# Eight more idle matmuls on TensorE in the first block of a gated linear attention with a bilinear feed-forward

## The chip, the core and the metric

The kernel runs on one core of a Trainium2 chip. A core has five engines, each with its own instruction queue: TensorE (PE in the profile; its weight loads are PEld), VectorE (DVE), ScalarE (ACT), GpSimd (POOL) and SyncE (SP). The metric is the device time of one execution in microseconds (us), as the median of several runs. The profile shows one execution on its own.

## The reference

Gated linear attention over 4 batch rows, 8 heads, 768 steps and a head size of 48 comes first, then a bilinear feed-forward layer over the 3072 tokens with a model size of 384 and an inner size of 1536. `alpha` lies between 0.8 and 1.

```python
state = np.zeros((B, H, D, D))
for t in range(S):
    state = alpha[:, :, t, :, None] * state + np.einsum('bhd,bhe->bhde', k[:, :, t], v[:, :, t])
    y[:, :, t] = np.einsum('bhd,bhde->bhe', q[:, :, t], state)
x = y.transpose(0, 2, 1, 3).reshape(B * S, H * D)
out = (x @ w_a) * (x @ w_b) @ w_out
```

## The kernel before

The steps in time are cut into three stretches of 256 steps and the batch into two pairs of rows. So there are six blocks, numbered 0 to 5; block c has stretch c // 2 and the pair c % 2. Each block runs through the same stages for its two rows (u = 0 and 1):

- load alpha, q, k, v (`load`, line 547), logarithm of alpha on ScalarE (`ln`, line 554)
- running sums of the logarithms over the steps, by matmuls with a triangular matrix (`B`, lines 589 and 590, for block 0), and sums over half stretches for the decay of the state (`dk`, line 698)
- exponentials of the sums and of the negated sums on ScalarE (`E`, line 665), multiplied into q and k on VectorE (`mq`, `mk`, line 676)
- transposes of q and k on TensorE (`C`, line 736) and the copy of the result out of PSUM (`Ce`, line 960)
- scores of keys and queries (`D`, line 837), masked on VectorE (`M`, line 846) or copied by ScalarE and masked afterwards (`Mc`, line 850, and `Mm`, line 854)
- the state that is carried on: matmuls of keys and values (`K`, line 792) and its update with the decay on VectorE (`k`, lines 819 to 823); the decays are made by ScalarE (`de`, line 719)
- the output: carried part from the state (`SB`, `SA`) and inner part from the masked scores (`Y`), all through line 866, then the evacuation to `xT` (`X`, lines 902 and 904)
- feed-forward: `a` and `b` are the products with w_a and w_b (line 921), `as` copies one of them out on ScalarE (line 927), `pr` multiplies them on VectorE (line 935), `o` is the product with w_out (line 943); the last blocks use a scheme with fewer products (line 1032)

Values of the logarithm and the running sums of block 0 are float32, so their matmuls run as two passes each. Blocks overlap: while one is in its feed-forward part, the next is in its attention part.

The order of all work is written out by hand in the string `PROGRAM`. Each entry is an operation, with its arguments and, where there is a choice, the engine's letter (V is VectorE, S ScalarE, P GpSimd, Y SyncE). The loop at line 1142 issues them in this order, and each engine keeps it in its own queue, so an operation that must wait holds up all that stands behind it on the same engine. For matmuls one of the arguments is the number of the PSUM bank, 0 to 7, that they write; two-bank operations take the next one as well.

The operation `fill n i` (line 570) issues n matmuls of a 128x128 block of zeros with 128x512 zeros into bank i. Nothing reads what they write; a real operation overwrites it later. The tile of zeros, `wz`, is set once at the start. In the kernel before there are two places with such fills: seven at the very start, before alpha has landed, and two in block 0 between the transposes `C 0 1 3` and `C 0 0 1`. `B 0b`, `B 0a`, `B 1a` and `B 1b` are the running sums of block 0: row 0 or 1, each for half of the heads (a is heads 0 to 3, b is heads 4 to 7).

The loads of all weights (`W`, line 527, and `Wo`, line 530) and those of q, k, v and alpha marked P are issued by GpSimd, one behind the other and between its own work; those marked Y by SyncE.

Of the kernel before, what the change touches and what calls it, by code (L numbers as in the profile page):

```python
# [17 lines left out]
0: cm 0; c1; cz 0 b P; ci; ld a 0b Y; c1a; ld a 0a Y; ln 0b; cu; cz 1 b P; fill 7 0; cu2 V  # L18
0: cz 0 q V; cus; ld k 0b Y; ld k 0a Y; B 0b 2; ld q 0b Y; ln 0a; B 0a 0; ld v 0 P; ld q 0a Y; ld a 1 P; cs 0 m P
0: E 0b i; mk 0b V; ld k 1 P; ld q 1 P; cm 1; W b 0 256; cz 0 v P; E 0b b; mq 0b V; ld v 1 P; W a 256 768; dk 0 2  # L20
0: C 0 1 3; E 0a i; mk 0a V; cz 1 q P; E 0a b; mq 0a V; v 0 S; Ce 0 1 V; fill 2 0; W a 0 256; de 0; W b 256 512
0: C 0 0 1; Ce 0 0 V; D 0 1 2; K 0 0 0; vs 0 0 S; W b 512 768; cs 1 m P
1: ld a 0 P
0: D 0 0 4; k 0 0 V; SB 0 0; M 0 0; ln 1; B 1a 6
1: ld a 1 P
0: W a 768 1536; c2 P; W b 768 1536; E 1a i; E 1a b; B 1b 4
1: ld q 0 P
# [1150 lines left out]
```

## Time and profile before

| | us |
|---|---|
| median of 3 runs | 189.28 |
| the three runs | 189.28, 190.45, 189.12 |
| the profiled execution, own time | 190.44 |
| its span, from first to last instruction | 188.7 |
| PE busy | 181.9 |
| DVE busy | 152.6 |
| ACT busy | 120.1 |
| POOL busy | 53.6 |
| mean granted clock of TensorE | 0.991 |

In the rows of a timeline the columns are start and duration in us, engine, line, operation, output and inputs, shape and count, and in brackets the idle time of the engine before it with what ended it. In the chain of waits a row is a piece of the path that ended last: start, duration, engine, tile and line. A matmul's duration includes the time until its last result is out, so that matmuls in a row overlap in their rows. In a row on a transfer the last number is the time in us from its issue to its landing.

### The profile page before, as it was taken

To read this page: it belongs to the slowest core of one execution; us is meant where nothing else is said; L and a number is where in the kernel's file an instruction comes from. 1 tells how busy PE (TensorE), PEld (TensorE's weight loads), DVE (VectorE), ACT (ScalarE), POOL (GpSimd) and SP (SyncE) were. 2 spreads that over 40 slices of the span, in tenths; PEclk is the share of its full clock that TensorE was granted. 3 is DMA by queue.
4 is the path that set the end of the run, shared out by engine and by line. 5 is a ranking of instruction groups with operands and counts; after the bars stand their busy time and mean duration, and the time that the engine had idled before them with its cause. 6 is when DMAs were issued, how large, how long until landed. Compare 5 with 4: busy or idle time off the path is not lost.

```text
span 188.7 us, 6347 instructions
## 1 busy us (share of the span) xinstructions
PE 181.9 (96%) x2693; PEld 122.3 (65%) x2709; DVE 152.6 (81%) x271; ACT 120.1 (64%) x228; POOL 53.6 (28%) x74
## 2 busy tenths in 40 slices
PE   7979999999999999999999999999999999999993
PEld 3969886566778886754445644555457477565992
DVE  2484889788979799998889899999999945696862
ACT  4364865579995797797697949965980451526230
POOL 8999654998062240003500003300000000000000
PEclk9987999999999999999999999999999999999999
DMA  5999999999999899989999699939500102110053
GB/s 125 263 225 195 261 235 254 230 231 257 247 214 129 129 215 276 275 237 182 198 173 271 144 116 167 112 107 165 89 0 9 43 0 83 44 43 0 0 170 127
DMA packets 66285, 29.43 MB, mean 156 GB/s; under 512 B 55776, under 2 KB 64624, under 8 KB 66256
## 3 DMA queue, kind: packets, MB, share of 16 engines
q1 hardware_dynamic: 47488, 16.34, 41.2%
q0 software_dynamic: 18624, 12.58, 39.3%
q8 instruction: 21, 0.34, 0.7%
q10 hardware_dynamic: 144, 0.10, 0.2%
q14 instruction: 8, 0.07, 0.1%
HBM read 25.98 MB, written 4.74 MB: 163 GB/s over the span
## 4 chain that ended last, share of the span: by engine, by line
PE 90%; ACT 6%; issue 2%; DVE 1%
PE psum L921 47%; PE psum L943 12%; PE psum L1032 11%; PE psum L866 5%; PE psum L837 3%; PE psum L589 2%; PE psum L590 2%; PE psum L736 2%; PE psum L572 2%; ACT vx L958 2%; PE psum L631 1%; ACT la L554 1%; PE psum L792 1%; PE psum L805 1%; PE psum L698 1%
## 5 line engine op out<-in xcount | busy, mean ns | idle before, releaser
L921 PE MATMUL psum<-xT,wb_t 128*128 128x512 bf16 (+1 forms) x263 | 55.8, 336 | 0.5 <-issue 0.2
L921 PE MATMUL psum<-xT,wa_t 128*128 128x512 bf16 (+1 forms) x262 | 55.2, 335 | 0.5 <-issue 0.2
L921 PEld LDWEIGHTS <-wa_t 128*128 128x128 bf16 x270 | 25.7, 98 | 19.2 <-issue 0.5
L921 PEld LDWEIGHTS <-wb_t 128*128 128x128 bf16 x270 | 25.5, 98 | 18.4 <-issue 0.5
L943 PE MATMUL psum<-wo_t,prod 128*128 128x384 bf16 x144 | 26.1, 327 | 0.0
L958 ACT ACTIVATE ot<-psum 128x384 f32<-128x384 f32 (+1 forms) x23 | 11.2, 487 | 17.7 <-PE psum L1032 15.4
L650 POOL TENSOR_TENSOR q_t<-q_t,ra 128x384 f32<-128x384 f32 x6 | 6.4, 1072 | 53.6 <-ACT ra L643 31.1
L943 PEld LDWEIGHTS <-prod 128*128 128x128 bf16 x144 | 13.3, 98 | 8.3
L958 ACT ACTIVATE vx<-v_t 32x384 bf16<-32x384 bf16 x26 | 13.5, 521 | 1.5 <-DVE vx L771 1.1
L1032 PEld LDWEIGHTS <-prod 128*128 128x128 bf16 x144 | 12.0, 98 | 1.2
L850 ACT ACTIVATE m<-psum 128x768 bf16<-128x768 f32 x14 | 11.0, 810 | 2.3 <-PE psum L837 2.3
L676 DVE TENSOR_TENSOR QKp<-q_t,beta 128x768 bf16<-128x768 f32 x10 | 9.4, 952 | 1.9 <-ACT beta L665 1.6
L554 ACT ACTIVATE la<-a_t 128x1536 f32<-128x1536 f32 (+2 forms) x9 | 9.5, 1054 | 1.7 <-DMA a_t<-in_alpha_dram 1.5
L676 DVE TENSOR_TENSOR QKp<-k_t,invb 128x768 bf16<-128x768 f32 x10 | 10.1, 1013 | 0.3
L846 DVE TENSOR_TENSOR m<-psum,mask 128x768 bf16<-128x768 f32 x10 | 9.5, 949 | 0.6 <-PE psum L837 0.6
L1044 DVE TENSOR_TENSOR ot<-psum,ot 128x384 f32<-128x384 f32 x9 | 5.0, 555 | 5.9 <-issue 3.2
L866 PE MATMUL psum<-m,vx 64*64 64x128 bf16 (+1 forms) x576 | 8.7, 205 | 0.0
L547 POOL DMA_DIRECT2D v_t<-in_v_dram x8 | 8.5, 1064 | 0.0
L866 PE MATMUL psum<-kqT,Sm 64*64 64x128 bf16 x144 | 7.5, 220 | 0.4 <-DVE Sm L819 0.4
L866 PEld LDWEIGHTS <-vx 64*64 64x64 bf16 x576 | 7.6, 108 | 0.1
L854 DVE TENSOR_TENSOR m<-m,mask 128x768 bf16<-128x768 bf16 x14 | 7.4, 550 | 0.0
L665 ACT ACTIVATE prod<-psum 128x384 f32<-128x384 f32 x8 | 3.5, 488 | 6.0 <-PE psum L590 6.0
(292 smaller groups left out, 361.5 us busy)
## 6 DMA issues: line engine op xcount, KB each, us to landing
out_dram<-ot SPq DMA_DIRECT2D x23, 192.0 KB, 2.7
q_t<-in_q_dram SPq DMA_DIRECT2D x3, 768.0 KB
k_t<-in_k_dram SPq DMA_DIRECT2D x3, 768.0 KB
a_t<-in_alpha_dram POOLq DMA_DIRECT2D x2, 768.0 KB, 11.7
v_t<-in_v_dram POOLq DMA_DIRECT2D x4, 384.0 KB, 7.6
a_t<-in_alpha_dram SPq DMA_DIRECT2D x2, 768.0 KB
a_t<-in_alpha_dram POOLq DMA_DIRECT2D x3, 384.0 KB, 7.5
k_t<-in_k_dram POOLq DMA_DIRECT2D x3, 384.0 KB, 7.3
```

The costliest lines, as they stand in the source:

```text
L547: eng.dma_start(out=t[:, us, hs].rearrange("p b h r d -> p (b h) (r d)"), in_=src[ch.b0 + us.start:ch.b0 + us.stop, hs, ch.s * 2 * C:(ch.s ...
L554: nc.scalar.activation(out=ch.la[:, us, hs].rearrange("p b h r d -> p (b h r d)"), in_=ch.a[:, us, hs].rearrange("p b h r d -> p (b h r d) ...
L650: eng.tensor_mul(x, x, by)
L676: eng.tensor_mul(QKp[ch.c % 2][:, u, j, :, hs, :D], src[:, u, hs].rearrange("p h r d -> p r h d"), f)
L846: nc.vector.tensor_mul(m, x, maskn())
L850: nc.scalar.activation(out=m, in_=x, func=AF.Copy)
L854: eng.tensor_mul(m, m, maskn())
L866: nc.tensor.matmul(o, lhsT=lhsT, rhs=rhs, start=(g, c) not in begun, stop=False, skip_group_check=True)
L921: nc.tensor.matmul(p, lhsT=(wa_t, wb_t)[w][:, kk, f * 128:(f + 1) * 128], rhs=ch.xT[:, kk, us, :], start=(kk == 0), stop=(kk == KT - 1))
L943: nc.tensor.matmul(op, lhsT=ch.prod[:, f, at:at + C], rhs=wo_t[:, f, :], start=(f == 0), stop=(f == NFF - 1))
L958: nc.scalar.activation(out=o_, in_=i_, func=AF.Copy)
L1032: nc.tensor.matmul(o[:, g], lhsT=A[:, f, g * C:(g + 1) * C], rhs=W[:, f], start=(not more and (apart or g == 0) and f == 0), stop=(f == LH ...
```

## The change

One of the two earlier fills in block 0 grows from two matmuls to three, and three new fills are put in: three matmuls into bank 0 ahead of the first scores (`D 0 1 2`), two into bank 6 ahead of the first carried sums (`SB 0 0`), two into bank 6 ahead of the second row's running sums (`B 1a 6`).

```diff
-0: C 0 1 3; E 0a i; mk 0a V; cz 1 q P; E 0a b; mq 0a V; v 0 S; Ce 0 1 V; fill 2 0; W a 0 256; de 0; W b 256 512
-0: C 0 0 1; Ce 0 0 V; D 0 1 2; K 0 0 0; vs 0 0 S; W b 512 768; cs 1 m P
+0: C 0 1 3; E 0a i; mk 0a V; cz 1 q P; E 0a b; mq 0a V; v 0 S; Ce 0 1 V; fill 3 0; W a 0 256; de 0; W b 256 512
+0: C 0 0 1; Ce 0 0 V; fill 3 0; D 0 1 2; K 0 0 0; vs 0 0 S; W b 512 768; cs 1 m P
 1: ld a 0 P
-0: D 0 0 4; k 0 0 V; SB 0 0; M 0 0; ln 1; B 1a 6
+0: D 0 0 4; k 0 0 V; fill 2 6; SB 0 0; M 0 0; ln 1; fill 2 6; B 1a 6
 1: ld a 1 P
```

The function that each of them calls:

```python
def fill(n, i):
    for _ in range(n):
        nc.tensor.matmul(bank(i), lhsT=wz[:, :C], rhs=wz, start=True, stop=True)
```

## The prediction

> **What bounds the kernel now.** I read the page first, then the clock in windows, then the chain of waits from 5 to 17 us, then the timelines of single engines. The page:
>
> ```profile
> span 188.7 us, 6347 instructions
> ...
> PE 181.9 (96%) x2693; PEld 122.3 (65%) x2709; DVE 152.6 (81%) x271; ACT 120.1 (64%) x228; POOL 53.6 (28%) x74
> ...
> PEclk9987999999999999999999999999999999999999
> DMA  5999999999999899989999699939500102110053
> ...
> PE 90%; ACT 6%; issue 2%; DVE 1%
> ```
>
> The matrix engine carries 90% of the chain that ends last. Its clock is full except in the third and fourth slices (9.4 to 18.9 us). The DMA row says that the transfers are also near their limit from about 5 to 85 us: two resources run side by side. The windows of 3.41 us that end at the clock's two changes:
>
> ```profile
> 0.00:2.49 2.49, 1.30 (x4) 0.48 (x5) 0.40 (x4) 1.28 (x1) 1.69 (x12) 1.00 0.18 33
> 2.49:5.90 3.41, 3.41 (x11) 2.17 (x10) 0.91 (x4) 1.05 (x2) 3.34 (x7) 1.00 1.01 246
> 5.90:9.31 3.41, 3.41 (x53) 3.05 (x54) 2.01 (x4) 1.75 (x4) 3.18 (x7) 1.00 1.39 259
> 9.31:12.73 3.42, 2.10 (x64) 1.70 (x64) 2.87 (x6) 2.97 (x6) 3.38 (x6) 1.00 1.05 243
> 12.73:16.14 3.41, 3.41 (x12) 3.41 (x12) 1.56 (x4) 0.80 (x2) 3.41 (x6) 0.50 1.54 190
> ```
>
> Columns: window, then busy time (and count) of PE, PEld, DVE, ACT, POOL, then granted clock, DMA share, GB/s. PE is busy for 2.10 of 3.42 us from 9.31 to 12.73, and exactly in the next 3.41 us the clock is 0.50. During that time PE is busy throughout, and by its end the clock is back. So a thinly filled window is followed by a slow one. (The 1.00 of the first two rows stands ahead of the first recorded change; the pairs below show that those matmuls were slow as well.) What lies in the slow window is on the chain:
>
> ```profile
> 5.14 0.64 PE psum L590 x2
> ...
> 6.23 0.33 PE psum L590 x2
> ...
> 11.63 0.85 ACT la L554
> 12.49 0.04 issue
> 12.53 0.85 PE psum L589 x2
> 13.39 0.64 PE psum L590 x2
> ...
> 16.75 0.33 PE psum L590 x2
> 17.08 0.84 PE psum L698 x32
> ```
>
> One pair of running-sum matmuls takes 0.64 us before 5.9 us and between 13.4 and 16, and 0.33 us at full clock. Block 0's second row has eight such pairs, from 12.53 to 17.08: 4.55 us. At full clock they would take 8 x 0.33 = 2.64 us, 1.91 us less.
>
> **The change part by part.** It adds eight 128x512 matmuls of zeros: one more behind the transposes of heads 4 to 7, three ahead of D 0 1 (first scores), two ahead of SB 0 0 (first carried sums), two ahead of B 1a (second row's running sums). Nothing is removed or moved, and no DMA, POOL or SP instruction is touched. The first four write bank 0 and the others bank 6; both were last used by PE itself or read by ScalarE well before, so I see no new wait of a fill on another engine. Their price, and the slots into which they fall:
>
> ```profile
> 33.31 1.47 PE L921 MATMUL psum<-xT,wa_t 128*128 128x512 bf16 x6
> 34.62 1.46 PE L921 MATMUL psum<-xT,wb_t 128*128 128x512 bf16 x6
> 9.51 0.61 PE L736 MATMUL psum<-ident,QKp 128*128 128x128 bf16 x8
> 10.58 0.34 PE L837 MATMUL psum<-kqT 64*64 64x128 bf16 x13 [0.46 <-ACT bl L719]
> 11.80 0.35 PE L866 MATMUL psum<-kqT,Sm 64*64 64x128 bf16 x6 [0.43 <-DVE Sm L819]
> 12.53 0.85 PE L589 MATMUL psum<-la,ut 128*128 128x192 f32 x2 [0.37 <-ACT la L554]
> ```
>
> Six matmuls of the same shape start every (34.62 - 33.31) / 6 = 0.218 us at full clock, so eight cost 1.75 us of PE time. The idle slots there hold 0.46 + 0.43 + 0.37 = 1.26 us. Step by step:
> - The third fill ahead of C 0 0 moves these transposes from 9.51 to 9.73. DVE's copy Ce 0 0 and D 0 0 follow by as much.
> - C 0 0 then ends at 9.73 + 0.61 = 10.34 by its row, which includes the last one's run-out. Three fills end at 10.34 + 0.65 = 10.99. If the run-out overlaps the fills it is some 0.15 earlier. D 0 1 stood at 10.58, so it starts 0.25 to 0.4 later; I take 0.3. Queued behind it on PE are K 0 0 (whose result makes Sm on DVE) and D 0 0.
> - The carried sums move from 11.80 to 12.10. The two fills ahead of them take 0.44, about the 0.43 in which PE waited for Sm, so they hide there. Without that cover they would cost 0.44.
> - The carried sums then end at 12.10 + 0.35 = 12.45, and two fills end at 12.65 (run-out hidden) to 12.9. The running sums stood at 12.53, when the logarithms came. So the delay is 0.12 to 0.37; I take 0.25.
>
> PE would then be busy for nearly all of 9.31 to 12.73, like 5.90 to 9.31, which was followed by full clock. If that holds the clock, the running sums end 1.91 - 0.25 = 1.66 us earlier. Bounds on this first effect: 0.12 to 0.37 lost if the clock drops all the same, 1.79 gained at best.
>
> [...]
>
> **What of the 1.66 us reaches the end.** From 18 us on PE has almost no gaps, so an earlier PE stays earlier until it waits for data. The loads are issued from POOL back to back and land at the pace of the transfer queues, which faster matmuls don't change. The two that come closest:
>
> ```profile
> 18.30 0.79 POOL L527 DMA_DIRECT2D wb_t<-in_moe_w_b_dram  x1
> wb_t<-in_moe_w_b_dram POOLq DMA_DIRECT2D x1, 576.0 KB, 12.0
> 31.34 1.79 PE L921 MATMUL psum<-xT,wb_t 128*128 128x256 bf16 x9
> 34.82 1.18 POOL L547 DMA_DIRECT2D a_t<-in_alpha_dram  x1
> a_t<-in_alpha_dram POOLq DMA_DIRECT2D x1, 768.0 KB, 10.8
> 45.90 1.49 ACT L554 ACTIVATE la<-a_t 128x1536 f32<-128x1536 f32 x1
> 45.90:50.49 4.59, 4.59 (x104) 3.24 (x103) 4.36 (x10) 4.49 (x6) 0.48 (x1) 1.00 1.14 252
> 50.64 0.81 ACT L902 ACTIVATE xT<-psum 128x768 bf16<-128x768 f32 x1 [0.15 <-PE psum L866]
> 50.97 1.15 PE L943 MATMUL psum<-wo_t,prod 128*128 128x384 bf16 x6
> 51.96 0.82 PE L921 MATMUL psum<-xT,wa_t 128*128 128x256 bf16 x6
> ```
>
> - The second half of w_b lands at 18.30 + 12.0 = 30.3. Its first use is the second third of the nine matmuls at 31.34, so about 31.7. An earlier start by more than 1.4 us waits there: 1.66 becomes 1.4.
> - Block 2's alpha lands at 34.82 + 10.8 = 45.6, and ScalarE takes its logarithm at 45.90, only 0.3 us later. ScalarE works in order and is busy for 4.49 of the next 4.59 us. So the evacuation X 0 of block 1 (50.64) cannot start before 45.7 + 4.59 = 50.29, ends at 51.10, and the feed-forward matmuls at 51.96 cannot start before 51.15. This leaves PE at most 0.81 us ahead, and ScalarE itself only 0.28. I take the middle, 0.55 us.
>
> What is late next is therefore ScalarE behind block 2's logarithm, with PE waiting up to 0.85 us for it around 50 us.
>
> The sum for the profiled execution, whose own time is 190.44 us (1.7 us more than its span): 190.44 - 0.55 = 189.9. It lies 1.16 us above the median of 189.28 (runs from 189.12 to 190.45), so it is at the slow end. Against the median: 189.28 - 0.55 = **188.7 us**.
>
> **The rivals.**
> - *All of it is kept* (0.17): PE finds other work or the loads land earlier. For it: the chain names PE for 90% of the span and no load there. Against it: the arithmetic of 45.6 us. 189.28 - 1.66 = 187.6, at best 187.5.
> - *The fills do nothing for the clock in the timed runs* (0.27): either the activity that counts isn't PE's busy time, so that the clock drops at 12.73 as before, or the slow window falls elsewhere in most executions and only the profiled one paid it. For it: two of three times are 1.2 us under the profiled one. Against it: the lost gain would be hidden at 45.6 us in those runs as well, so that the spread need not be the clock. It costs 0.12 to 0.37 us, less what a drop saved in some runs returns: 189.3 to 189.6, say 189.4. [...]
> - *Slower: the drop moves* (0.10): the new wait before 51.15 leaves up to 0.85 us of a 3.41 us window idle, and if thin small matmuls around it count for little, the clock halves from about 52 on. The price is half of 3.41, 1.7 us; less the 0.81 that PE was ahead, +0.9: 190.2. It decides once a window there is filled to no more than the 61% that brought the drop before. Against it: 0.85 idle of 3.41 is still 75% busy. With two such windows it would be +2.6, 191.9.
>
> **How the numbers follow.** The forecast has 0.40; the cases above 0.54; 0.06 stay for what I have not seen, more of it slower. The forecast's own range, from gains of 0.28 to 0.81, is 188.5 to 189.0. The range for 8 in 10 takes in most of the full gain below and the moved drop above: 187.5 to 190.3. A difference of 1%, 1.9 us, is about what a measurement of this kernel can tell from no change. Faster by more (under 187.4) needs the whole gain with the delay at its lower bound, and a median before that paid for the slow clock: 0.13. Slower by more (over 191.2) needs two slow windows or something unseen: 0.10. Within 1%: 0.77.
>
> **What would show it.** Right: the granted clock 1.00 from 12.73 to 16.14; eight pairs of 0.33 us; the running sums at 12.65 to 12.9 and decay sums (17.08 before) near 15.4; ScalarE's logarithm of block 2 at 45.6 to 45.7 with a wait for alpha ahead of it; PE idle somewhere between 49 and 52. Wrong: the clock at 0.50 after 12.73, PE without a gap and still 1.6 us ahead at 55 us, alpha landing earlier than 45.6, or a new slow window anywhere after 20 us.

## The result and the profile after

| | before | after |
|---|---|---|
| median of 12 runs, us | 189.24 (188.72 to 190.45) | 190.34 (189.72 to 191.77) |
| ratio, after to before | | 1.0066 [1.0040, 1.0092] |
| the profiled execution, own time | 190.44 | 190.52 |
| its span | 188.7 | 188.7 |

The change costs 0.66%, 1.1 us. The forecast was a gain of 0.55 us, 188.7, in a range from 187.5 to 190.3. The result lies just above its upper end, on the other side of no change.

The two profiled spans are equal, although the medians are not. So the two traces differ by something that was won and lost again. First the page of the kernel after:

```profile
span 188.7 us, 6362 instructions
...
PE 182.6 (97%) x2700; PEld 121.9 (65%) x2717; DVE 153.5 (81%) x271; ACT 120.1 (64%) x228; POOL 52.2 (28%) x74
...
PEclk9999999999999999999999999999999999999999
...
PE 88%; ACT 4%; issue 2%; DMA 1%; DVE 1%; SPq 1%
```

The clock row has no slow slice any more. But a transfer (DMA 1%) and SyncE's queue (SPq 1%) have come into the chain, which had neither before. What was won stands in the windows that were shown of before, with the same columns (busy time and count of PE, PEld, DVE, ACT, POOL, then granted clock, DMA share, GB/s):

```profile
9.31:12.73 3.42, 3.21 (x70) 2.04 (x70) 2.52 (x6) 2.86 (x7) 3.42 (x6) 1.00 1.07 246
12.73:16.14 3.41, 3.41 (x25) 2.96 (x24) 3.09 (x6) 0.87 (x2) 3.41 (x5) 1.00 1.55 192
```

PE is busy for 3.21 us of the first window instead of 2.10, and the clock in the second is 1.00 instead of 0.50. The chain of waits of the kernel after, around the running sums (start, duration, what):

```profile
12.43 0.38 PE psum L572
12.81 0.28 PE psum L866 x6
13.10 0.54 PE psum L572 x2
13.63 0.33 PE psum L589 x2
...
15.91 0.33 PE psum L590 x2
16.23 0.84 PE psum L698 x32
```

The eight pairs take 0.33 us each, 2.60 us together, where they took 4.55. But they start at 13.63 and not at 12.53, because the fills (line 572) now stand in the chain themselves. They end at 16.23 instead of 17.08: 0.85 us won. The kernel after stays some 0.7 us ahead up to 128 us. Then it waits, as the chain shows:

```profile
130.51 1.01 SPq L687
131.52 0.06 issue
131.58 2.68 DMA bl<-row
134.27 1.04 issue
135.31 0.06 DVE Sm L823
135.37 0.41 issue
135.78 0.60 DVE prod L935
136.40 0.96 DVE m L846
137.39 0.36 PE psum L866 x12
```

This is the update of block 5's state. `bl` holds the decays, which SyncE loads from DRAM (line 687); VectorE makes `Sm` from them (line 823), and PE's matmuls at line 866 stand behind the work that VectorE then has in its queue. The same place in VectorE's timeline, of before:

```profile
134.45 0.54 DVE L822 TENSOR_TENSOR tmp<-psum,S 128x384 f32<-128x384 f32 x1
135.03 0.56 DVE L823 TENSOR_TENSOR Sm<-tmp,bl 128x384 bf16<-128x384 f32 x1
```

And of after:

```profile
133.71 0.54 DVE L822 TENSOR_TENSOR tmp<-psum,S 128x384 f32<-128x384 f32 x1
135.31 0.56 DVE L823 TENSOR_TENSOR Sm<-tmp,bl 128x384 bf16<-128x384 f32 x1 [1.05 <-issue]
```

`tmp` begins 0.74 us earlier than before, `Sm` 0.28 us later. Before, the second step followed the first at once; now 1.05 us of waiting lie between them. That takes the lead away in this pair of executions. The questions are why a median without a slow clock is the better one, and what eight matmuls of zeros at 12 us have to do with a transfer at 131 us.

### The profile page after: what moved, and what is told of

It reads as the page before. It is cut to its first block, busy times and chain, and to the rows that moved or that the text cites. A ratio compares the mean times of both kernels' runs of the same rounds, so it can differ in the third digit from the quotient of the medians.

```text
span 188.7 us, 6362 instructions
## 1 busy us (share of the span) xinstructions
PE 182.6 (97%) x2700; PEld 121.9 (65%) x2717; DVE 153.5 (81%) x271; ACT 120.1 (64%) x228; POOL 52.2 (28%) x74
## 4 chain that ended last, share of the span: by engine, by line
PE 88%; ACT 4%; issue 2%; DMA 1%; DVE 1%; SPq 1%
PE psum L921 44%; PE psum L943 12%; PE psum L1032 11%; PE psum L866 5%; PE psum L572 3%; PE psum L837 3%; PE psum L736 2%; PE psum L589 2%; PE psum L590 2%; DMA bl<-row 1%; PE psum L698 1%; PE psum L631 1%; PE psum L792 1%; ACT vx L958 1%; PE psum L805 1%
## 5 line engine op out<-in xcount | busy, mean ns | idle before, releaser
L665 ACT ACTIVATE beta<-psum 128x384 f32<-128x384 f32 x10 | 4.8, 494 | 3.7 <-PE psum L636 3.6
```

## The experiments

In the expectations below, theory letters stand for readings that were weighed as the runs came in. A: the slow clock was an accident of the one profiled execution, and the fills cost what they delay. B: the drop is the rule, the fills do remove it, and more is lost elsewhere. C: the length of TensorE's program moves a code load into block 5's decay load. D: the fills' time, or their effect on the clock, brings the loss. E: more instructions cost as such, wherever they stand. F: the code load costs in another way than through the decay load. Each kernel was run 12 times; a time is the median, and the ratio is to the kernel before on the same chip, with its 95% interval. Program length is counted in instructions of TensorE: a bf16 matmul is two, its weight load and itself, so the change adds 16 (the two pages show 8 weight loads more, 2717 for 2709, and 7 matmuls, 2700 for 2693; one of the eight has no record). Where an expectation counts rows of the program, it takes a float32 matmul as one.

### The kernel before once more, the change, and its two halves

The kernel before, unchanged:

> The unchanged kernel, for a second profile and the granted clock of each of its executions. Theory A (the slow clock after 12.73 us was an accident of the one profiled execution, at 190.45 us the slowest of 12): most executions show a mean clock of 0.997 to 1.000, and the new profile has no stretch at 0.50 between 9 and 20 us, with a span near 187.5 us. Theory B (the drop is the rule and the fills do remove it, but over 2 us are lost elsewhere): most executions show 0.991, and the profile has the stretch at 0.50.

189.15 us, 0.9998 [0.9978, 1.0018], profiled span 187.4, so 1.3 us shorter than that of the first profile. The windows of this execution:

```profile
9.31:12.73 3.42, 3.12 (x74) 2.36 (x72) 3.08 (x6) 2.75 (x6) 3.38 (x6) 1.00 1.10 240
12.73:16.14 3.41, 3.41 (x75) 3.17 (x77) 3.08 (x8) 1.91 (x6) 3.41 (x6) 1.00 1.53 188
```

The kernel before doesn't drop its clock here, and the first window is filled for 3.12 us without any new fill. (The edges are those of the first profile. There the clock first rose at 5.90 us, here at 6.96.) Each run comes with its mean granted clock; the first profile had 0.991. Of all 140 executions of the kernel before that were made beside these experiments, 10 had 0.991 or less, the others 0.997 to 1.0. A mean of 0.991 is what 3.41 us at half clock make of a span of 188.7; where the slow stretch lay in those executions no trace shows. The ten took from 190.62 to 193.52 us, with a median of 191.0, against 189.1 to 189.2 for the others. So the drop costs about 1.8 us, near the 1.91 that the prediction gave it, but it comes in 7 of 100 executions (from 1 of 47 on one chip to 4 of 23 on another), and the first profile was of that kind. Removing it is worth some 0.07 x 1.8 = 0.13 us on the average, an estimate.

The chain of the same profile shows a second thing:

```profile
12.24 6.94 DMA wa_t<-in_moe_w_a_dram
19.17 0.05 issue
19.22 1.48 PE psum L921 x12
```

The first feed-forward matmul waits for w_a until 19.17 us. In this execution what stands in block 0 ahead of that has slack.

All eight fills, the kernel after:

> All eight fills. Both theories: ratio 1.004 to 1.009, 190.0 to 190.6 us. Theory A: compared with the new profile of the kernel before, the second row's running sums start 0.1 to 0.4 us later, and the rest of the 1.1 us is a wait behind it. Theory B: they end 1.5 us or more earlier, and the loss lies at waits for transfers after 60 us.

190.51 us, 1.0072 [1.0050, 1.0094], span 188.1, clock 1.00. By the timelines its running sums start at 12.77 instead of 12.18, but its feed-forward starts at 19.13, where it started at 19.22: the fills' time goes into the wait for w_a. From 21 us on ScalarE's instructions run, but for a few short stretches, 0.00 to 0.09 us ahead of e1_before's up to 135.8 us, and 1.03 behind from 137.5. In the last 10 us 0.39 us come back, because e1_before has its own wait there, for a slot of the output store. So in this pair the loss lies at the state update of block 5 alone. The pair isn't an even one, though: the clock first rose at 5.60 us in e1_after and at 6.96 in e1_before. In the first profile of after and in e3_after below it rose at 7.08 and 6.70, and the feed-forward starts at 19.83 and 19.63. There the fills' own time isn't hidden.

The first four fills alone, ahead of the second transposes and of the first scores:

```diff
-... Ce 0 1 V; fill 2 0; W a 0 256; ...
-0: C 0 0 1; Ce 0 0 V; D 0 1 2; ...
+... Ce 0 1 V; fill 3 0; W a 0 256; ...
+0: C 0 0 1; Ce 0 0 V; fill 3 0; D 0 1 2; ...
```

> Only the first four fills: the third one ahead of C 0 0 and the three ahead of D 0 1; none ahead of the carried sums and of the second row's running sums. Theory A (the fills cost what they delay; the scores move by 0.25 to 0.4 us, but the running sums wait for the logarithms and hide it): ratio 0.999 to 1.003. Theory B: between the kernel before and all eight, 1.002 to 1.006, with the clock held.

189.03 us, 0.9993 [0.9968, 1.0019]. The last four alone, ahead of the carried sums and the running sums:

```diff
-0: D 0 0 4; k 0 0 V; SB 0 0; M 0 0; ln 1; B 1a 6
+0: D 0 0 4; k 0 0 V; fill 2 6; SB 0 0; M 0 0; ln 1; fill 2 6; B 1a 6
```

> Only the last four fills, two ahead of the first carried sums and two ahead of the second row's running sums. Theory A (a fill ahead of the running sums delays them by what does not fit into the slot): 0 to 0.2 us, ratio 1.000 to 1.004. If the whole 1.1 us comes from these four, 1.004 to 1.009.

189.11 us, 0.9999 [0.9972, 1.0025]. Neither half shows a cost (the intervals leave room for up to 0.5 us), both together cost 0.7%. That doesn't look like a sum of costs of places. Something seems to jump between eight instructions more and sixteen.

### Time without instructions, instructions without time

The pages list packets of instructions beside those of data. From the page of the kernel after, its three largest queues (packets, MB, share of 16 engines):

```profile
q1 hardware_dynamic: 47488, 16.34, 41.2%
q0 software_dynamic: 18624, 12.58, 39.1%
q8 instruction: 21, 0.34, 0.8%
```

21 packets of 16 KB in one execution, each of 0.9 to 1.3 us in this trace. The trace names no engine for them. That they are TensorE's code is the author's estimate, from the counts: 2693 matmuls and 2709 weight loads of before are 5402 instructions, 257 for each of the 21 packets that its page has too, and from the first packet (at 13.62 us) to the last (at 179.83) TensorE starts 250 instructions from one to the next on the average, with single gaps of 45 to 390. If that is so, the microsecond in which such a block of code is fetched should depend on how many instructions stand ahead.

The first test keeps the time of eight fills and makes the program shorter than the change does. Fills in float32 take longer per instruction (by their rows, one of 384 columns takes 0.86 us as two matmuls in the trace of e2_f32, and three bf16 ones of 512 take 0.81 in that of e1_after); `zf` is a float32 view of the tile of w_out, which VectorE sets to zero at the start:

```diff
-... cz 1 b P; fill 7 0; cu2 V
+... cz 1 b P; fill 3 0; fillf 512 0; cu2 V
-... Ce 0 1 V; fill 2 0; W a 0 256; ...
-0: C 0 0 1; Ce 0 0 V; D 0 1 2; ...
+... Ce 0 1 V; fillf 384 0; W a 0 256; ...
+0: C 0 0 1; Ce 0 0 V; fillf 384 0; D 0 1 2; ...
-0: D 0 0 4; k 0 0 V; SB 0 0; M 0 0; ln 1; B 1a 6
+0: D 0 0 4; k 0 0 V; fill 2 6; SB 0 0; M 0 0; ln 1; fill 2 6; B 1a 6
...
+    def fillf(w, i):
+        nc.tensor.matmul(bank(i)[:, :w], lhsT=zf[:, :C], rhs=zf[:, :w], start=True, stop=True)
```

> All eight fills in time, but with TensorE's program one row shorter than before the change (5178 against 5179; all eight as the change has them make 5195): float32 fills, one row each for the time of four or three bf16 ones. Theory C (the loss comes from the length of TensorE's program ahead of block 5: one of its 16 KB code loads falls into block 5's decay load and holds up its last values by about 1 us): ratio 0.998 to 1.002, no wait of over 0.5 us ahead of the state update near 135 us, the code load behind the decay load's last value. Rival D (the fills' time or their effect on the clock moves the attention ahead of the transfers and the loss follows): 1.004 to 1.009, with the wait.

189.6 us, 0.9994 [0.9961, 1.0028]. The count in the expectation was wrong: a float32 matmul stands in the trace as two weight loads and two matmuls, so that the fills are 26 instructions against 18 before, eight more, as in either half. The run still tells the two apart: the time of eight fills with eight instructions is not slower by the ratio. Its median is 0.45 us higher, so a small cost of the fills' time isn't excluded.

The opposite: no new fill, only the seven first fills of the kernel cut into more and narrower ones, 15 of 239 columns instead of 7 of 512. They stream as many columns (3585 against 3584), with 16 instructions more:

```diff
-... cz 1 b P; fill 7 0; cu2 V
+... cz 1 b P; fillw 15 239 0; cu2 V
...
+    def fillw(n, w, i):
+        for _ in range(n):
+            nc.tensor.matmul(bank(i)[:, :w], lhsT=wz[:, :C], rhs=wz[:, :w], start=True, stop=True)
```

> The kernel before without any of the eight fills, but its seven first fills cut into fifteen of 239 columns (3585 columns for 3584): the same time at the start, and TensorE's program longer by the same 16 rows as with the change (5195). Theory C: the same loss as the change, ratio 1.004 to 1.009, and a wait of about 1 us ahead of the state update near 135 us, with a code load that starts 1 to 1.5 us earlier against the decay load than in the kernel before. Rival D: 0.998 to 1.002.

189.92 us, 1.0029 [0.9998, 1.0060]: the interval just holds no change. But the wait is there, in VectorE's timeline of this kernel (lines are 4 higher):

```profile
133.28 0.53 DVE L826 TENSOR_TENSOR tmp<-psum,S 128x384 f32<-128x384 f32 x1
134.88 0.56 DVE L827 TENSOR_TENSOR Sm<-tmp,bl 128x384 bf16<-128x384 f32 x1 [1.07 <-issue]
```

Sixteen instructions ahead of everything, with no added time, bring a wait of 1.07 us at the same place. Twice as many, 23 fills of 156 columns (`fillw 23 156 0`, 32 more), were to carry the fetch past the transfer:

> The kernel before with its seven first fills cut into 23 of 156 columns: program longer by 32 rows (5211). Theory C: the code load comes another 1 to 1.5 us earlier, near the start of the decay load or ahead of it, so the wait is under 0.4 us: ratio 0.998 to 1.003. If a longer program as such were the cost: more than with 16 rows, over 1.008. Rival D: 0.998 to 1.002.

190.89 us, 1.0080 [1.0049, 1.0111], with a wait of 0.95 us. And the eight fills of the change with `fillw 15 239 0`, also 32 more:

> All eight fills, and the seven first ones cut into fifteen of 239 columns: program longer by 32 rows (5211). Theory C: as with 32 rows and no fills, the collision is gone: ratio 0.998 to 1.003. Rival D: 1.004 to 1.009 as with the change.

191.54 us, 1.0106 [1.0074, 1.0138], with 0.76 us. (The profiled execution of this kernel is the fastest of its twelve, 189.73, so its trace doesn't show what the median lost.) Both missed what was expected: the wait doesn't go away with 32 instructions. That more instructions cost something holds, that the fetch slides on evenly with their number doesn't.

### Instructions ahead of the transfer and behind it

If the fetch at 132 us does it, then the place of the added fills doesn't matter as long as it is ahead of 130 us, and behind it they do nothing. Eight very small matmuls of zeros (64x64x64) at two places:

```diff
-5: a 4 * 3
+5: tiny 8 3; a 4 * 3
...
+    def tiny(n, i):
+        for _ in range(n):
+            nc.tensor.matmul(bank(i)[:DP, :DP], lhsT=wz[:DP, :DP], rhs=wz[:DP, :DP], start=True, stop=True)
```

That is at some 143 us, behind the transfer:

> The kernel before plus eight 64x64x64 matmuls of zeros (16 instructions of TensorE) ahead of block 5's first-layer products of chunk 4, about 143 us, behind block 5's decay load; their own time is at most 8 x 0.06 = 0.5 us. Theory C (the place of the code loads against block 5's decay load decides): ratio 0.999 to 1.003, no wait near 135 us. Theory E (16 more instructions cost as such, wherever they stand): at least 1.003 plus their own time, 1.004 to 1.008.

189.47 us, 1.0022 [0.9997, 1.0047]. Its VectorE:

```profile
132.75 0.54 DVE L826 TENSOR_TENSOR tmp<-psum,S 128x384 f32<-128x384 f32 x1
133.38 0.56 DVE L827 TENSOR_TENSOR Sm<-tmp,bl 128x384 bf16<-128x384 f32 x1
```

And ahead of it, at some 110 us in block 3's feed-forward (with the same `tiny`):

```diff
-3: b 9 * 4; b 5 * 3; a 4 * 5
+3: b 9 * 4; b 5 * 3; tiny 8 5; a 4 * 5
```

> The same eight matmuls in block 3's feed-forward, about 110 us, ahead of block 5's decay load and behind the whole start. Theory C: the wait of 0.7 to 1.1 us at block 5's state update near 135 us, ratio 1.003 to 1.008. If the loss arises at the start instead: 0.999 to 1.003, and no wait.

190.25 us, 1.0055 [1.0036, 1.0074]. Its VectorE:

```profile
133.47 0.53 DVE L826 TENSOR_TENSOR tmp<-psum,S 128x384 f32<-128x384 f32 x1
134.98 0.56 DVE L827 TENSOR_TENSOR Sm<-tmp,bl 128x384 bf16<-128x384 f32 x1 [0.97 <-DVE tmp L826]
```

(The releaser in the bracket is the step before, which had ended long ago; the wait is for `bl`.) The small matmuls take some time of their own on the chain of this run:

```profile
110.55 0.37 PE psum L576 x8
```

Those behind the transfer take time as well, and the two medians still differ by 0.78 us. So sixteen instructions some 100 us away from the places of the change bring its wait, and behind the transfer they don't. Half as many, 11 fills of 326 columns at the start (`fillw 11 326 0`, eight instructions more):

> The kernel before with its seven first fills cut into eleven of 326 columns: eight instructions more, no time more. Theory C: as with either half of the change (eight instructions more), 0.998 to 1.002, no wait near 135 us. If the loss grows evenly with the length: about 1.0015 to 1.004.

188.86 us, 0.9985 [0.9961, 1.0010], no wait. It has the lowest median of all, but its interval holds no change. The change itself beside these, once more:

> All eight fills once more, for a third profile and as the mark for this group: 1.005 to 1.009, with a wait of 0.7 to 1.1 us at block 5's state update near 135 us.

190.35 us, 1.0056 [1.0037, 1.0076], with a wait of 1.19 us.

The table is worked out from the packets of the profiles: when the code block's fetch starts after the issue of the decay load, how long the load takes from its first to its last value, and the gap between `tmp` and `Sm`, all in us.

| kernel | instructions more ahead of it | fetch starts at | load takes | gap |
|---|---|---|---|---|
| before, first profile | 0 | 4.16 | 2.14 | 0.03 |
| before, e1_before | 0 | 3.68 | 1.76 | 0.03 |
| first four fills | 8 | 3.69 | 2.42 | 0.25 |
| last four fills | 8 | 3.48 | 2.02 | 0.03 |
| float32 fills | 8 | 3.74 | 1.81 | 0.03 |
| 11 narrow fills | 8 | 3.90 | 2.12 | 0.03 |
| small ones behind it | 0 | 3.87 | 2.24 | 0.09 |
| after, first profile | 16 | 2.13 | 2.86 | 1.05 |
| after, e1_after | 16 | 2.13 | 3.09 | 1.28 |
| after, e3_after | 16 | 2.70 | 3.10 | 1.19 |
| small ones ahead of it | 16 | 2.23 | 2.78 | 0.97 |
| 15 narrow fills | 16 | 2.28 | 3.01 | 1.07 |
| 23 narrow fills | 32 | 2.18 | 2.81 | 0.95 |
| eight fills and 15 narrow ones | 32 | 2.16 | 2.62 | 0.76 |

The groups don't overlap in any column. With up to eight instructions more, the fetch comes when the load's last packet has landed, or in the two halves of the change 0.4 and 0.2 us ahead of that (the first half has the gap of 0.25); with 16 and more it falls into the load's midst. The load is some 1,600 packets of 4 bytes, and it is only just in time without a disturbance: in e1_before its last packet lands at 133.10 and `tmp` ends at 133.39, where `Sm` starts. So a delay of more than some 0.3 us is a delay of VectorE. The DMA queues from the load's first packet to its last, of e1_before (packets, MB, share of 16 engines):

```profile
q1 hardware_dynamic: 1841, 0.23, 85.5%
```

Of e1_after:

```profile
q1 hardware_dynamic: 1838, 0.23, 50.0%
q8 instruction: 1, 0.02, 2.6%
```

The same packets, and one more, the code block. The first stretch is 1.8 us long, the second 3.1. In the packets the last value lands at 133.1 us in the one and at 134.4 in the other, while `tmp` starts at 132.85 in both. The difference is in the load's end: by 133.10 all 1,616 packets of 4 bytes have started in e1_before and 1,561 in e1_after; 48 of e1_after's start only when the code packet has ended (133.38), the last one alone at 134.41. In the other six profiles with 16 or 32 instructions more, 52 to 221 packets start behind the code packet's end; in the seven with fewer there is none. Which of the 16 DMA engines carried which packet the record doesn't say.

### The load taken out of the fetch's way

If the collision is the cause, the change must become harmless when the decay load is issued earlier, with all eight fills in place. Block 5's load is given to GpSimd, which is free then and issues it at about 125 us, without SyncE's two transposes in front of it:

```diff
-5: vs 1 0 S; T 1; dl
+5: vs 1 0 S; T 1; dl * P
...
-    def decay_load(ch, us):
+    def decay_load(ch, us, eng):
...
-            nc.sync.dma_start(out=bls[ch.c % 2][r * DP:r * DP + D, us].rearrange("d b g a -> d (b g a)"),
+            eng.dma_start(out=bls[ch.c % 2][r * DP:r * DP + D, us].rearrange("d b g a -> d (b g a)"),
```

> All eight fills and TensorE's program as with the change, but block 5's decay load is issued by GpSimd, which is idle then, as soon as its rows are in DRAM (about 126 us) instead of by SyncE behind two transposing transfers (about 130.5 us). Theory C (the lateness of the decay load, held up by the code load, makes the loss): no wait ahead of the state update near 135 us, 0.7 to 1 us less than the change: ratio 0.998 to 1.003. Rival F (the code load costs in another way, as when TensorE lacks instructions or other transfers are held up): 1.004 to 1.009, the gap near 135 us stays on some engine.

189.57 us, 1.0012 [0.9984, 1.0040], where the change without this edit had ratios of 1.0066, 1.0072 and 1.0056 in its own three measurements. VectorE of this kernel:

```profile
133.75 0.54 DVE L822 TENSOR_TENSOR tmp<-psum,S 128x384 f32<-128x384 f32 x1
134.33 0.56 DVE L823 TENSOR_TENSOR Sm<-tmp,bl 128x384 bf16<-128x384 f32 x1
```

The decays have landed by 131 us here (the second issue at 125.62, at most 5.4 us to its landing). A code block is still fetched from 133.1 on, but the state update doesn't wait. GpSimd's queue also carries this load in another form, as 64 packets in place of some 1,600; whether the earlier issue or the fewer packets do it isn't told apart. The kernel before with the same edit, as a control:

> The same move of block 5's decay load, without fills. There was no wait to remove near 135 us, so both theories: 0.998 to 1.002.

189.94 us, 1.0017 [0.9979, 1.0054]. So the edit isn't a gain in itself. It takes the loss out of the change, most of it at least, and leaves the kernel before where it was.

The trace of the change with the moved load also shows a second place. At 113 us ScalarE's copy `kp` waits for a transposing transfer of block 4 (`kqT`), and the feed-forward stands behind it:

```profile
106.79 5.97 DMA kqT<-QKp
...
112.78 0.09 ACT kp L958
...
113.74 0.59 ACT as__2426 L927
...
114.37 2.75 PE psum L921 x12
```

In e1_before the chain runs through matmuls there. Set against e1_before, ScalarE falls back by 0.43 us at this place, and likewise in e3_after (0.46) and with the 15 narrow fills (0.39). In these three a code block is fetched 3.9 to 4.0 us behind the issue of that transfer, in most others 1.2 to 3.2. But the first profile of after has its fetch at 3.9 us too and loses nothing there, so that a second collision of the same kind is likely and not shown.

## Why the prediction was wrong

**The base: the drop was taken for the rule.** The prediction built its gain on the 1.91 us of a slow clock from 12.73 to 16.14. The amount was right (the ten executions that had the drop were about 1.8 us longer), but 130 of 140 executions of the kernel before don't have it. The text had the sign in hand: the profiled execution was 1.16 us above the median, and two of three times lay at the median or below. It let the wait at 45.6 us explain that away. The rival "the fills do nothing for the clock in the timed runs", 189.4, had this right and should have been the forecast, though it had no term for the loss either. That the slower rival's 190.2 comes near the result is luck: no clock dropped.

The step from a thinly filled window to a slow clock was taken from one trace, and it doesn't hold as a rule. In the profile of the 23 narrow fills the clock first rose at 4.39 us, and the windows of 3.41 us from there on read:

```profile
7.80:11.22 3.42, 1.96 (x45) 1.52 (x45) 2.28 (x4) 1.58 (x5) 3.26 (x7) 1.00 1.19 285
11.22:14.63 3.41, 2.61 (x57) 2.34 (x47) 2.69 (x5) 1.72 (x4) 3.41 (x6) 1.00 1.40 202
```

PE is busy for 1.96 us of the first, less than the 2.10 of the first profile, and the clock stays at 1.00. (In both windows one fill has no record, which makes each up to 0.2 us fuller.) So PE's busy share alone doesn't decide; what does, the runs don't tell. That the fills hold the clock isn't refuted: no execution of the kernels with all eight fills whose clock is on record, 60 in all, fell below 0.997, where 7 of 100 would be four. It is a matter of 0.13 us.

**The delay by the fills, 0.25 (0.12 to 0.37).** Mis-sized, and not one number. In the kernel before the running sums start 0.05 us behind the logarithms that they wait for (12.53 behind 12.48, in e1_before 12.18 behind 12.13). In the kernel after they start 1.23, 0.48 and 0.36 us behind them (first profile, e1_after, e3_after). The slots of PE in which the fills were to hide depend on when the clock first rises: 5.90 us in the profile of before, and 5.60, 6.70 and 7.08 in e1_after, e3_after and the first profile of after, where the sums start at 12.77, 13.27 and 13.47 by the timelines. With full speed coming later PE is behind its inputs there, and no slot is left. In the six profiles for which the first rise is given here it lies between 4.39 (23 narrow fills) and 7.08 us. In e1_before against e1_after the delay ends in the wait for w_a at 19.2 us, which the prediction didn't have as a gate.

**The gain cut at 45.6 us by block 2's alpha.** This didn't happen. In the kernel after ScalarE takes the logarithm earlier, without a wait:

```profile
45.22 1.48 ACT L554 ACTIVATE la<-a_t 128x1536 f32<-128x1536 f32 x1
```

The prediction had the loads issued at a pace of their own. But GpSimd issues them between steps that wait for the other engines (the row of alpha's issue stands at 33.59 instead of 34.82), and alpha had landed at 44.3 by the transfer's record. What bounded the gain wasn't the load. It was the fills' own delay. That the profile of after is 0.74 us ahead at `tmp`, not far from the forecast's 0.55, is luck. (The lower bound of 0.28 us also doesn't come out of the rows that it names: 45.90 less 45.7 is 0.20.)

**"No DMA, POOL or SP instruction is touched."** True, and the step that cost the sign. The change does touch DMA traffic, by the program that has to be fetched. Sixteen instructions of TensorE move the fetch of one code block into the decay load of block 5, from 3.5 to 4.2 us behind its issue to 2.1 to 2.7. In the five profiles with sixteen more, and the load in its place, VectorE waits for 0.97 to 1.28 us there, and ScalarE falls back by 0.7 to 1.0 us against e1_before; the section on the changed parts had no term for it. The slower rival, a drop that moves to 52 us, didn't take place.

**What stays open.** In e1 the two profiled executions differ by 0.66 us (189.88 and 189.22), which the trace accounts for: 1.03 lost at the state update, 0.39 won back in the tail. The medians differ by 1.36, and the other executions have no trace. The wait at 113 us and the fills' own time where the clock rises late can fill that gap; how often they come wasn't seen. With 32 instructions more 1.7 and 2.4 us are lost, though the wait at 135 us isn't longer in their profiles. In that of the 23 narrow fills ScalarE is 1.1 us behind e1_before from 25 us on already, after a later logarithm (it ends at 12.82 instead of 12.13); why stays open. By what rule the fetch's place jumps from about 3.7 to about 2.2 us behind the issue, rather than sliding, the runs don't tell. And the fills' own time may cost a few tenths (the float32 fills' median, and the 0.3 us that the medians leave to the change with the moved load).

## What to carry to other kernels

A single profile that lies above the median can show something that most runs don't have: here it was 1.16 us above, 0.6%, and 130 of 140 executions didn't have its slow stretch. So look at the granted clock of several runs before a gain is built on one. Where small packets land just in time, adding instructions ahead of them can cost as much as adding work: here sixteen made VectorE wait for 0.97 to 1.28 us at one load, in narrow fills at the start and in small matmuls at 110 us as well. Compare the instruction queue's packets with the tight transfers, and give a transfer without slack an earlier issue (with that the change had a ratio of 1.0012, without it 1.0056 to 1.0072). When a change loses time far away from its place, halve it: two halves that show no cost each (0.9993 and 0.9999) and a whole that shows one (1.0072) point to a jump and not to a sum of costs.

## What the hardware showed that was not expected

- One 16 KB packet of code among some 1,600 packets of 4 bytes lengthened their load from 1.8 to 3.1 us (e1_before and e1_after). No wait of TensorE in the chains here is put down to such a fetch, although the code is taken to be its own; the transfer under way at the time lost 1.3 us.
- The granted clock differs between executions of one kernel: 10 of 140 had a mean of 0.991 or less, with the same instructions. PE's busy share of a window doesn't foretell it: 1.00 came after a window of 1.96 us in 3.42, 0.50 after one of 2.10.
- A float32 matmul is two weight loads and two matmuls in the trace: in before, the 8 calls of line 589 stand as 16 of each. Whether it takes twice the room in the program too wasn't measured.
